# Decode step with attention and MLP on one core: the last 64 rows of w1 are fetched in another order of rows

## The chip, the core and the metric

The kernel runs on one core of a Trainium2 chip. The metric is device time of one execution in microseconds (us). Five compute queues matter: TensorE (PE, with its weight loads PEld), VectorE (DVE), ScalarE (ACT), GpSimd (POOL) and SyncE (SP), which here issues nearly all transfers. 16 DMA engines move the data.

## What is computed

```python
xn = layernorm(x)                                  # x: 4 x 576, bf16
A  = attention(xn, k_cache, v_cache, wq, wo)       # 32 query heads, 16 KV heads, the last 2048 positions of the cache
h  = gelu(layernorm(xn) @ w1)                      # w1: 576 x 576
g  = four quarters of h, each shifted along the sequence, joined
x1 = xn + g @ w2                                   # w2: 576 x 576
B  = x1 + gelu(layernorm(x1) @ w3) @ w4            # w3: 576 x 4608, w4: 4608 x 576
out = x + A + B
```

There are four batch rows, each with one position. With one position the shifts move everything out, so the joined quarters are zeros (`hs_inT` is a tile of zeros), and the product with w1 is computed though nothing reads its values.

## The kernel before

The data are 32 MB of K, 32 MB of V (16 transfers of 2 MB each) and the weights. The order on each queue is written out by hand: every operation is added with a key, and an engine's operations run in the order of their keys (`add`, `add_dma`, `emit_program`). Waits are on semaphores; each transfer adds 16 to its own one when it is complete, and w1's two transfers share one that must reach 32.

SP issues in this order (line 202 issues all of them): wq in two transfers (512 rows, then the last 64), w1 in two, w2 in two, w3 in two, w4 in two pieces (lines 268 to 276), then K 0 and 1, then K 2 once the query projection is done (`q`, line 358), K 3 (K 4 and later wait until a slot is free), then 15 pieces of V, the last of V, and wo in five pieces of 12, 10, 7, 2 and 1 rows a partition. All run through one queue of the 16 DMA engines.

Each weight with 576 rows is split. The first 512 rows lie four to a partition. The last 64 rows are cut in halves, so that 128 partitions get one half row each: `rag_src` (line 204) views rows 512 to 575 as 128 rows of half the width, half row 2r + h to partition 2r + h. For w1 a half row is 288 elements of bf16, 576 bytes, and the tile is `w1rag`. The other operand must match this layout: after each layernorm (`ln_ops`) two copies on DVE (lines 314 and 315) spread the last 64 elements of the normalized row over `ragsrc`, to the even places for h = 0 and to the odd places for h = 1, zeros elsewhere. TensorE transposes them (line 325), and `pe_hh` (line 393) multiplies them with `w1rag` behind the four products of the first 512 rows. Index 0 of `ragsrc` belongs to wq, 1 to w1, 2 to w3.

The attention then works on one K transfer at a time: transposes on TensorE (line 496), copies out of PSUM on DVE and ACT (480, 479), scores (503); then softmax, the transposed probabilities (530 to 543), the products with V (567) with their folding (573 to 591), and the output projection with wo (386, 64 matmuls at the end), which is copied out on DVE and ACT (628, 629).

Of the kernel before, what the change touches and what calls it, by code (L numbers as in the profile page):

```python
# [34 lines left out]
def bass_parallel_sum__sliding_block_cached__mixer_s_mlp__decode_kernel(  # L35
    nc, A_x, A_k_cache, A_v_cache, A_wq, A_wo, B_x, B_w1, B_w2, B_w3, B_w4, out
):
    B, Sq, D = A_x.shape
# [25 lines left out]
    with ExitStack() as ctx:  # L64
        def sb(name, shape, dt):
            return ctx.enter_context(nc.sbuf_tensor(name, shape, dt))

        def sem(name):
            return ctx.enter_context(nc.semaphore(name))
# [20 lines left out]
        def cut(n):  # L90
            nonlocal _o
            _o += n
            return ktb[:, _o - n:_o]
        w1main = cut(4 * D).rearrange("p (r n) -> p r n", r=4)
        w1rag = cut(HALF)
# [22 lines left out]
        ragsrc = sb("ragsrc", [B, 3, 2, 128], BF16)  # L118
# [72 lines left out]
        def add(engine, emit, waits=(), sig=None, key=0.0, inc=None):  # L191
            seqc[0] += 1
            prog[engine].append(Op(emit, waits, sig, key, seqc[0], inc))

        def add_dma(pairs, skey, waits=(), key=0.0, engine="sp"):
            if skey not in S:
                S[skey] = sem("s_" + "_".join(str(k) for k in (skey if isinstance(skey, tuple) else (skey,))))
            dma_count[skey] = dma_count.get(skey, 0) + 16 * len(pairs)

            def emit(e):  # L200
                for o_, i_ in pairs:
                    e.dma_start(o_, i_).then_inc(S[skey], 16)  # L202
            add(engine, emit, waits, None, key)
            return ("dma", skey, dma_count[skey])

        def rag_src(w_ap):
            return w_ap[512:576, :].rearrange("r (h n) -> (r h) n", h=2)

        for n in range(NB):
            ev_val[f"T{n}"] = ("T", n + 1)  # L210
        for c in range(-1, NC - 1):
# [51 lines left out]
        for x in range(2):  # L263
# [3 lines left out]
        ev_x = add_dma([(x_sb[:], x2)], "x", (), -100, engine="act")  # L267
        ev_wq = [add_dma([(kring[:, 2 * UE:4 * UE], A_wq[0:512, :].rearrange("(p r) n -> p (r n)", r=4))], "wq", (), -50),
                 add_dma([(wqrag, rag_src(A_wq))], "wqr", (), -49)]
        ev_w1 = add_dma([(w1main, B_w1[0:512, :].rearrange("(p r) n -> p r n", r=4)), (w1rag, rag_src(B_w1))], "w1", (), -48)  # L270
        ev_w2 = add_dma([(w2main, B_w2[0:512, :].rearrange("(p r) n -> p r n", r=4)), (w2rag, rag_src(B_w2))], "w2", (), -47)
        ev_w3 = add_dma([(vring[:, 0:4 * F], B_w3[0:512, :].rearrange("(p r) n -> p (r n)", r=4)), (w3rag, rag_src(B_w3))],
                        "w3", (), -46)
# [17 lines left out]
        ev_wo, WOR, a = [], [], 0  # L291
# [10 lines left out]
        def ln_ops(idx, src, dst, first_waits, tag, k0):  # L302
            add("dve", lambda e: (e.bn_stats(out=stats[:, idx, 0, :], in_=src[:, 0:HALF]),
                                  e.bn_stats(out=stats[:, idx, 1, :], in_=src[:, HALF:D]))[1],
                waits=first_waits, sig=f"{tag}_st", key=k0)
            add("dve", lambda e: e.bn_aggr(out=mv[:, idx, :], in_=stats[:, idx].rearrange("p a s -> p (a s)")),
                waits=[f"{tag}_st"], sig=f"{tag}_mv", key=k0 + 0.01)
            add("act", lambda e: e.activation(out=sd[:, idx:idx + 1], in_=mv[:, idx, 1:2], func=ACTF.Sqrt, bias=EPS, scale=1.0),
                waits=[f"{tag}_mv"], sig=f"{tag}_sd", key=k0 + 0.02)
            add("dve", lambda e: e.reciprocal(out=rstd[:, idx:idx + 1], in_=sd[:, idx:idx + 1]),  # L310
                waits=[f"{tag}_sd"], sig=f"{tag}_rstd", key=k0 + 0.03)
            add("dve", lambda e: e.tensor_scalar(out=dst[:], in0=src[:], scalar1=mv[:, idx, 0:1], scalar2=rstd[:, idx:idx + 1],  # L312
                                                 op0=ALU.subtract, op1=ALU.mult), waits=[f"{tag}_rstd"], sig=f"{tag}_n", key=k0 + 0.04)
            add("dve", lambda e: (e.tensor_copy(out=ragsrc[:, idx, 0, 0:128:2], in_=dst[:, 512:D]),
                                  e.tensor_copy(out=ragsrc[:, idx, 1, 1:128:2], in_=dst[:, 512:D]))[1],  # L315
                waits=[f"{tag}_n", "rag_zero"], sig=tag, key=k0 + 0.05)

        def pe_xT(src, idx):
            def f(e):
# [9 lines left out]
        def pe_zero(e):  # L329
# [3 lines left out]
            return ins  # L333

        ln_ops(0, x_sb, xn_bf, [ev_x], "ln1", -40)
        ln_ops(1, xn_bf, xn2_bf, ["ln1"], "ln2", -30)
        for idx, (src, tag, dst) in enumerate(((xn_bf, "ln1", xnT), (xn2_bf, "ln2", xn2T))):
            add("pe", pe_xT(src, idx), waits=["ident_bf", tag], sig=f"xT{idx}", key=-50 + idx)
            add("dve", lambda e, dst=dst, idx=idx: e.tensor_copy(out=dst[:], in_=XTps[idx]), waits=[f"xT{idx}"], sig=f"xnT{idx}",  # L339
                key=-29 + idx * 0.1)  # L340
# [36 lines left out]
        for k in range(2):  # L377
            for b in range(B):
                for g in range(2):
                    add("dve", lambda e, k=k, b=b, g=g: e.tensor_copy(  # L380
                            out=qp_out[:, b, 2 * k + g].rearrange("p (j n) y -> p j n y", j=2),
                            in_=QTps[:, k, :, 2 * g:2 * g + 2, b].rearrange("p (n y) j -> p j n y", y=2)),
                        waits=["qTp1", "qpad_zero"], sig=f"qT{8 * k + 2 * b + g}", key=-10 + 0.1 * k)
# [20 lines left out]
        for h in range(2):  # L404
            cs = slice(HALF * h, HALF * (h + 1))
            add("pe", pe_hs(h), waits=[ev_w2, "hs_inT"] + (["x1a"] if h else []), sig=f"hs{h}", key=-23 + h)
            add("dve", lambda e, cs=cs: e.tensor_tensor(out=x1_bf[:, cs], in0=HSps, in1=xn_bf[:, cs], op=ALU.add),
                waits=[f"hs{h}"], sig="x1" if h else "x1a", key=-7 + 0.1 * h)
        ln_ops(2, x1_bf, x1n_bf, ["x1"], "ln3", -6)
        add("dve", lambda e: e.tensor_tensor(out=t1[:], in0=x_sb[:], in1=x1_bf[:], op=ALU.add), waits=["x1"], sig="t1", key=-5.9)  # L410
        add("act", lambda e: (e.activation(out=hh_sb[0:B, :], in_=HHps[0], func=ACTF.Gelu_apprx_tanh),
                              e.activation(out=hh_sb[32:32 + B, :], in_=HHps[1], func=ACTF.Gelu_apprx_tanh))[1],
            waits=["hT", "ln3_sd"], sig="gelu_h", key=-5.9)
# [38 lines left out]
        for k in range(3):  # L452
            add("pe", pe_h2(k), waits=[ev_w3] + (["x1nT", "gelu_h", "h2_zero"] if k == 0 else []), sig=f"h2_{k}", key=-18 + k)
            add("act", lambda e, k=k: e.activation(out=h2_sb[:, k], in_=H2ps[k], func=ACTF.Gelu_apprx_tanh), waits=[f"h2_{k}"],
                sig=f"gelu2_{k}", key=-5 + 0.1 * k)
# [3 lines left out]
            waits=["h2Tp"], sig="h2T", key=-4.5)  # L459
# [17 lines left out]
        def evac(n):  # L477
            if n % 8 in ACT_EVAC:
                return "act", lambda e: e.activation(out=ktbuf[:, n % NKT], in_=tb[n % 4], func=ACTF.Copy)  # L479
            return "dve", lambda e: e.tensor_copy(out=ktbuf[:, n % NKT], in_=tb[n % 4])  # L480

        for n in range(NB):
            c, k = n // NBLK, n % NBLK
            if k == 0:
                add("dve", lambda e, c=c: e.tensor_copy(out=Qs[:, c % N_CB, :], in_=Qpad_t[:, 128 * (4 * CH[c][0] + CH[c][1]):][:, 0:128]),
                    waits=["qT15"] + ([f"SC{c - N_CB}"] if c >= N_CB - 1 else []), key=n)
            eng, f = evac(n)
# [11 lines left out]
        def emit_SC(e, k):  # L499
# [11 lines left out]
            waits=["rmax"], sig="negb", key=KS + 0.05)  # L511
        for q in range(4):
            add("act", lambda e, q=q: e.activation(out=P_sb[:, q, :], in_=Sps[:, q, :], func=ACTF.Exp,
                                                   bias=negb[:, 0:1], scale=scale, accum_out=rs4[:, q:q + 1]),
                waits=["negb"], sig=f"exp{q}", key=KS + 0.1 + 0.01 * q)
# [18 lines left out]
        for q in range(4):  # L534
            k0 = KS + 0.2 + 0.1 * q
            add("dve", dve_mask(q), waits=[f"exp{q}", "mask4"], sig=f"P4_{q}", key=k0)
            add("pe2", pe_PT(q), waits=[f"P4_{q}"] + (["sel_bf"] + [f"E{NB - 1 - k}" for k in range(4)] if q == 0 else []),
                sig=f"PTp{q}", key=k0)
            add("act", lambda e, q=q: e.activation(out=PTx[:, q, :], in_=ps[:, 4 + q, :], func=ACTF.Copy),  # L539
                waits=[f"PTp{q}"], sig=f"PTx{q}", key=k0 + 0.05)  # L540
            add("pe2", lambda e, q=q: e.matmul(ps[:, q, :], lhsT=permT_bf[:], rhs=PTx[:, q, :], start=True, stop=True),
                waits=[f"PTx{q}", "permT_bf"], sig=f"PTy{q}", key=k0 + 0.11)
            add("act", lambda e, q=q: e.activation(out=PT_t[:, 512 * q:512 * (q + 1)], in_=ps[:, q, :], func=ACTF.Copy),  # L543
                waits=[f"PTy{q}"], sig=f"PT{q}", key=k0 + 0.16)
# [3 lines left out]
            waits=["rinv", "ident_f"], sig="diag", key=KS + 0.82)  # L548
        add("pe2", lambda e: e.matmul(rinvps, lhsT=ones_f[:], rhs=diag[:], start=True, stop=True),
            waits=["diag", "ones_f", "PT3"], sig="rinvp", key=KV + 0.5)  # L550
        add("dve", lambda e: e.tensor_copy(out=rinvB[:].rearrange("p (c u e) -> p c u e", u=NU, e=2),
                                           in_=rinvps.rearrange("p (u c e) -> p c u e", u=NU, e=2)),
            waits=["rinvp"], sig="rinvB", key=KV + 1.5)
# [26 lines left out]
        for c in range(NC):  # L580
            b, gq = CH[c]
# [5 lines left out]
                waits=[f"PV{c}", "maskd"], key=KV + 2 * c + 0.6, inc=(("FF", k), 1))  # L587
            add("dve", lambda e, c=c: e.tensor_reduce(out=acc[:, c % NVS, :], in_=tmp[c % 2].rearrange("p t d -> p d t"), axis=AX.X, op=ALU.add),  # L588
                waits=[f"F{c}"] + ([f"fold{c - NVS}"] if c >= NVS else []), key=KV + 2 * c + 0.7, inc=(("AA", k), 1))
            cs = slice(32 * b + 8 * gq, 32 * b + 8 * gq + 8)  # L590
            add("dve", lambda e, k=k, cs=cs: e.tensor_tensor(out=OTn[:, cs], in0=OTps[k], in1=rinvB[:, cs], op=ALU.mult),  # L591
                waits=["rinvB", f"fold{c}"], key=KV + 2 * c + (2.75 if c < NC - 1 else 3), inc=(("OO", k), 1))
# [11 lines left out]
            waits=["OR"], sig="ORT", key=KE + 0.3)  # L604
# [66 lines left out]
        e = nc.tensor  # L671
# [62 lines left out]
```

## Time and profile before

| | us |
|---|---|
| median of 3 runs | 215.27 (215.07 to 215.28) |
| profiled execution | 215.12 |
| its span | 213.9 |

In the profile, busy time is the time in which an engine executes; for the DMA engines it is the mean share over all 16. "The chain that ended last" follows the work back from the last instruction, at each step to what released it. A stretch of the span lists each engine's busy time (with the number of instructions), the granted TensorE clock, the busy share of the DMA engines and the rate in GB/s. A DMA issue is listed with its size and the time from issue to landing. In counts of packets, those under 512 B are nearly all the small packets with which an engine reports its share of a transfer as done.

### The profile page before, as it was taken

How to read it: one execution, taken by the hardware profiler on the slowest of the kernel's cores; microseconds unless marked ns; L12 is line 12 of the kernel's file. 1: busy time of each engine (PE TensorE's matmuls, PEld its weight loads, DVE VectorE, ACT ScalarE, POOL GpSimd, SP SyncE). 2: the span in 40 equal slices, each digit the busy share in tenths (PEclk: the TensorE clock that was granted, in tenths of full speed). 3: DMA queues.
4: the chain of work that ended last, by engine and by line, in shares of the span. 5: the costliest groups of instructions: out<-in, count | busy, mean ns of one | idle time of the engine just before them, and what ended most of it. 6: DMA issues, size and time to landing. Idle time of an engine off the chain costs nothing.

```text
span 213.9 us, 4528 instructions
## 1 busy us (share of the span) xinstructions
PE 151.6 (71%) x1984; PEld 96.9 (45%) x1987; DVE 116.8 (55%) x240; ACT 64.3 (30%) x78; POOL 12.7 (6%) x20
## 2 busy tenths in 40 slices
PE   2038478578999999999999971788444455555964
PEld 0013126337878877888887860434111122212332
DVE  4962720015767776667677666759934333334520
ACT  2001032003666666556666665810000000000000
POOL 8950000000000000000000000000000000000000
PEclk9999958889999999999999999557855555555699
DMA  7999989999999999999999999999999999999993
GB/s 277 411 385 494 427 376 440 429 417 420 435 429 420 423 438 426 423 426 438 427 420 429 435 426 420 434 429 417 429 435 423 426 432 435 423 426 432 426 400 122
DMA packets 6802, 88.64 MB, mean 414 GB/s; under 512 B 764, under 2 KB 1160, under 8 KB 1928
## 3 DMA queue, kind: packets, MB, share of 16 engines
q1 hardware_dynamic: 6776, 88.50, 97.7%
q8 instruction: 7, 0.11, 0.2%
q14 instruction: 3, 0.02, 0.0%
q10 hardware_dynamic: 16, 0.01, 0.0%
HBM read 88.49 MB, written 0.00 MB: 414 GB/s over the span
## 4 chain that ended last, share of the span: by engine, by line
DMA 68%; PE 17%; DVE 9%; ACT 3%; issue 1%; SPq 1%
DMA kring<-in_A_k_cache_dram 41%; DMA kring<-in_A_wo_dram 16%; DMA vring<-in_A_v_cache_dram 10%; PE ps L496 7%; DVE xn_bf L312 4%; PE ps L567 3%; PE ps L503 2%; PE ps L358 2%; SPq L202 1%; DVE rmax L509 1%; DVE ktb L521 1%; ACT ktb L539 1%; ACT PT L543 1%; DMA x_sb<-in_A_x_dram 1%; PE ps L386 1%
## 5 line engine op out<-in xcount | busy, mean ns | idle before, releaser
L480 DVE COPY ktb<-ps 128x1024 bf16<-128x1024 bf16 x80 | 53.8, 690 | 24.7 <-PE ps L496 24.2
L496 PE MATMUL ps<-perm_bf,kring 128*128 128x128 bf16 x1024 | 62.6, 219 | 3.0 <-DMA kring<-in_A_k_cache_dram 2.1
L496 PEld LDWEIGHTS ps<-perm_bf,kring 128*128 128x128 bf16 x1024 | 57.2, 98 | 12.6 <-issue 9.8
L479 ACT ACTIVATE ktb<-ps 128x1024 bf16<-128x1024 bf16 x48 | 49.2, 1024 | 31.6 <-PE ps L496 30.8
L567 PE MATMUL ps<-vring,ktb 128*32 128x512 bf16 x240 | 25.8, 575 | 23.2 <-DMA vring<-in_A_v_cache_dram 23.2
L585 DVE TENSOR_TENSOR ktb<-ps,maskd 128x512 f32<-128x512 f32 x16 | 11.0, 690 | 29.6 <-PE ps L567 29.5
L629 ACT ACTIVATE out_sb<-ps 4x288 bf16<-4x288 f32 x1 | 0.4, 402 | 72.4 <-PE ps L386 72.4
L567 PEld LDWEIGHTS ps<-vring,ktb 128*32 128x32 bf16 x240 | 7.1, 121 | 30.9 <-issue 27.3
L503 PE MATMUL ps<-ktb,Qs 128*32 128x512 bf16 x272 | 17.8, 382 | 1.2 <-ACT ktb L479 1.2
L588 DVE TENSOR_REDUCE acc<-ktb 128x128 f32<-128x512 f32 x16 | 16.4, 1028 | 0.5
L573 PEld LDWEIGHTS ps<-sel,acc 128*128 128x128 f32 x34 | 7.3, 268 | 14.6 <-issue 8.8
L573 PE MATMUL ps<-sel,acc 128*128 128x8 f32 x34 | 8.8, 331 | 2.5 <-DVE OTn L591 2.5
L503 PEld LDWEIGHTS ps<-ktb,Qs 128*32 128x32 bf16 x272 | 5.8, 95 | 6.7 <-DVE ktb L480 1.4
L322 PE MATMUL ps<-ident_bf,xn_bf 4*128 4x4 bf16 x8 | 0.6, 170 | 11.4 <-DVE xnT L339 8.9
L386 PE MATMUL ps<-vring,h2T_sb 128*4 128x288 bf16 x72 | 6.4, 348 | 2.5 <-DMA vring<-in_B_w_dram 2.5
L559 DVE TENSOR_TENSOR ktb<-PT,mU_bf 128x512 bf16<-128x512 bf16 x16 | 6.6, 416 | 2.1 <-ACT PT L543 2.1
L312 DVE TENSOR_SCALAR xn_bf<-xn_bf,mv,rstd 4x576 bf16<-4x576 bf16 x1 | 7.4, 7430 | 0.0
L245 POOL MEMSET ktb<- 128x8192 bf16 x1 | 6.9, 6925 | 0.0
L530 PE MATMUL ps<-sel_bf,ktb 128*128 128x32 bf16 x64 | 2.4, 189 | 5.5 <-DVE ktb L521 5.5
L386 PE MATMUL ps<-kring,ORT 128*4 128x288 bf16 x64 | 4.4, 286 | 2.4 <-DMA kring<-in_A_wo_dram 1.8
L322 PEld LDWEIGHTS ps<-ident_bf,xn_bf 4*128 4x128 bf16 x8 | 0.4, 112 | 12.3 <-DVE ragsrc L315 9.0
L386 PEld LDWEIGHTS ps<-vring,h2T_sb 128*4 128x4 bf16 x72 | 3.6, 100 | 5.1 <-DMA vring<-in_B_w_dram 2.7
(117 smaller groups left out, 96.4 us busy)
## 6 DMA issues: line engine op xcount, KB each, us to landing
kring<-in_A_k_cache_dram SPq DMA_DIRECT2D x16, 2048.0 KB, 14.7
vring<-in_A_v_cache_dram SPq DMA_DIRECT2D x15, 2048.0 KB, 22.4
vring<-in_B_w_dram SPq DMA_DIRECT2D x1, 4608.0 KB, 24.9
kring<-in_A_wq_dram SPq DMA_DIRECT2D x1, 4096.0 KB, 12.4
vring<-in_B_w_dram SPq DMA_DIRECT2D x1, 3456.0 KB, 34.7
kring<-in_A_v_cache_dram SPq DMA_DIRECT2D x1, 2048.0 KB, 26.7
ktb<-in_B_w_dram SPq DMA_DIRECT2D x3, 576.0 KB, 14.5
vring<-in_B_w_dram SPq DMA_DIRECT2D x1, 1728.0 KB, 38.3
```

Source lines behind the costliest of these rows:

```text
L245: P(lambda e: e.memset(ktb[:, NKT // 2 * 1024:NKT * 1024], 0.0), key=-92, inc=(("E", LB - 2), 1))
L312: add("dve", lambda e: e.tensor_scalar(out=dst[:], in0=src[:], scalar1=mv[:, idx, 0:1], scalar2=rstd[:, idx:idx + 1], op0=ALU.subtract, op ...
L386: return e.matmul(ACC[h], lhsT=lhsT, rhs=rhs, start=start, stop=stop, tile_position=(0, 32 * h), skip_group_check=True)
L479: return "act", lambda e: e.activation(out=ktbuf[:, n % NKT], in_=tb[n % 4], func=ACTF.Copy)
L480: return "dve", lambda e: e.tensor_copy(out=ktbuf[:, n % NKT], in_=tb[n % 4])
L496: ins = e.transpose(tb[j % 4][:, t, :], kslot_t(k)[:, 8 * kb + t, :], perm_bf[:])
L503: ins = e.matmul(Sps[32 * u:32 * u + 32, q, :].rearrange("p (t i) -> p t i", t=16), lhsT=Qs[:, k, 32 * u:32 * u + 32], rhs=ktgrp[:, (4 * k ...
L559: return lambda e: e.tensor_tensor(out=PTpad[:, c % NVS], in0=PTv[:, :, cc, :].unsqueeze(2).to_broadcast([128, NT, NU, 2]), in1=mU_bf[:].u ...
L567: ins = e.matmul(ps[32 * j:32 * j + 32, PVb[k], :], lhsT=PTpad[:, k, 4 * g:4 * g + 4].rearrange("p t u e -> p (t u e)"), rhs=v[:, 512 * g: ...
L573: e.matmul(OTps[k], lhsT=acc[:, k, :], rhs=sel8[:], start=True, stop=True, skip_group_check=True).then_inc(S["FO"], 1)
L585: add("dve", lambda e, c=c: e.tensor_tensor(out=tmp[c % 2], in0=ps[:, PVb[c % NVS], :].rearrange("p (t d) -> p t d", t=4), in1=maskd[:].un ...
L588: add("dve", lambda e, c=c: e.tensor_reduce(out=acc[:, c % NVS, :], in_=tmp[c % 2].rearrange("p t d -> p d t"), axis=AX.X, op=ALU.add), wa ...
```

## The change

The source of w1's last 64 rows is viewed through one more rearrangement: the 128 half rows are taken as 16 groups of 8, and walked with the place in the group outermost (8), the group next (16), the 288 elements last. The destination is the same tile of 128 partitions. So partition 16a + b gets half row 8b + a. To match, the two copies that fill `ragsrc` for index 1 write the elements in the order of these half rows: for each h, 4 x 16 elements. Half row 8b + a is half h = a mod 2 of row 4b + a div 2, so each h reads its elements with a stride of 4 and writes runs of 16. Indices 0 and 2 are filled as before, and the transfers of all other weights stay.

```diff
+        def rag8_src(w_ap):
+            return rag_src(w_ap).rearrange("(b a) n -> a b n", a=8)
...
-        ev_w1 = add_dma([(w1main, B_w1[0:512, :].rearrange("(p r) n -> p r n", r=4)), (w1rag, rag_src(B_w1))], "w1", (), -48)
+        ev_w1 = add_dma([(w1main, B_w1[0:512, :].rearrange("(p r) n -> p r n", r=4)), (w1rag, rag8_src(B_w1))], "w1", (), -48)
...
-            add("dve", lambda e: (e.tensor_copy(out=ragsrc[:, idx, 0, 0:128:2], in_=dst[:, 512:D]),
-                                  e.tensor_copy(out=ragsrc[:, idx, 1, 1:128:2], in_=dst[:, 512:D]))[1],
-                waits=[f"{tag}_n", "rag_zero"], sig=tag, key=k0 + 0.05)
+            def rag(e):
+                ins = None
+                for h in range(2):
+                    if idx == 1:
+                        ins = e.tensor_copy(out=ragsrc[:, 1, h].rearrange("q (a x b) -> q x a b", a=4, x=2)[:, h],
+                                            in_=dst[:, 512:D].rearrange("q (b a) -> q a b", a=4))
+                    else:
+                        ins = e.tensor_copy(out=ragsrc[:, idx, h, h:128:2], in_=dst[:, 512:D])
+                return ins
+            add("dve", rag, waits=[f"{tag}_n", "rag_zero"], sig=tag, key=k0 + 0.05)
```

## The prediction

> **What bounds the kernel now.** I read the busy shares first, then the DMA queues, the chain that ended last, and the stretches by time.
>
> ```profile
> span 213.9 us, 4528 instructions
> PE 151.6 (71%) x1984; PEld 96.9 (45%) x1987; DVE 116.8 (55%) x240; ACT 64.3 (30%) x78; POOL 12.7 (6%) x20
> ...
> DMA packets 6802, 88.64 MB, mean 414 GB/s; under 512 B 764, under 2 KB 1160, under 8 KB 1928
> ## 3 DMA queue, kind: packets, MB, share of 16 engines
> q1 hardware_dynamic: 6776, 88.50, 97.7%
> ```
>
> No compute engine is above 71%. The queue that SP feeds (q1) keeps the 16 DMA engines busy for 97.7% of the span: the kernel is a stream of 88.5 MB. The chain of waits says the same: 68% of it is DMA, and its end is this.
>
> ```profile
> 150.30 20.86 DMA vring<-in_A_v_cache_dram
> ...
> 175.56 34.97 DMA kring<-in_A_wo_dram
> 210.54 0.04 issue
> 210.58 1.44 PE ps L386 x20
> 212.01 0.44 DVE out_sb L628
> ```
>
> The last transfers (wo) are issued at 174.5 to 176.5 and land some 35 us later, because they stand behind all that was issued before. So the end is set by how long an engine needs for its own share of everything queued. The stretches show how the 16 engines end (the last two columns are the busy share of the DMA engines and GB/s):
>
> ```profile
> 180.00:200.00 20.00, 11.28 (x76) 4.63 (x77) 8.33 (x16) 0.00 (x0) 0.00 (x0) 0.50 1.00 426
> 200.00:205.00 5.00, 4.08 (x31) 1.58 (x30) 2.27 (x5) 0.00 (x0) 0.00 (x0) 0.88 1.00 421
> ...
> 208.00:209.00 1.00, 0.83 (x14) 0.61 (x16) 0.00 (x0) 0.00 (x0) 0.00 (x0) 1.00 0.97 392
> 209.00:210.00 1.00, 0.56 (x10) 0.17 (x4) 0.00 (x0) 0.00 (x0) 0.00 (x0) 1.00 0.62 247
> 210.00:211.00 1.00, 0.42 (x8) 0.32 (x10) 0.00 (x0) 0.00 (x0) 0.00 (x0) 1.00 0.43 161
> 211.00:212.00 1.00, 0.97 (x16) 0.47 (x12) 0.00 (x0) 0.00 (x0) 0.00 (x0) 1.00 0.03 12
> ```
>
> Until 209 all are busy; then the share falls to 0.62 and 0.43. So about half of the engines are out of work near 209.5, and the others run to about 211. All engines have the same bytes, yet the late ones are some 1.5 us behind, and the kernel waits for them: PE starts its last 20 matmuls at 210.58, when the third piece of wo has landed on its slowest engine. A microsecond given to a late engine is a microsecond of the kernel; one given to an early engine costs nothing up to 1.5 us.
>
> **The change, part by part.**
>
> *The transfer's split.* The 128 rows of 576 B (72 KB) stay; the source is now walked as 8 x 16 rows. Do the shapes decide how many engines take part? The page's counts answer for the rows here. Every engine that takes part in a transfer posts a completion packet of a few bytes. The page lists 47 issues with 128 destination rows (16 of K, 16 of V, 5 of wo, 10 of the other weights) and 3 with 4 rows (x and two of out). 47 x 16 + 3 x 4 = 764, which is the page's count of packets under 512 B. So 128 rows went to 16 engines and 4 rows to 4. A transfer whose one side begins with 8 and the other with 128 does not occur here; I take it that the smaller side decides, and that 8 engines get 16 rows each where 16 had 8. [...]
>
> *The price of a row.* The stretch from 14.5 to 16 us holds this transfer whole:
>
> ```profile
> DMA packets 278, 0.62 MB, mean 412 GB/s; under 512 B 32, under 2 KB 160, under 8 KB 278
> ...
> q1 hardware_dynamic: 278, 0.62, 104.2%
> ```
>
> 160 - 32 = 128 are its rows, 32 are completions, and 118 are rows of 4608 B of w1 and w2. Their time is 1.042 x 16 x 1.5 us = 25.0 us. The stretch 16 to 16.5 holds only 47 rows of 4608 B at 104.6%, so 1.046 x 16 x 0.5 / 47 = 178 ns each. 25.0 - 118 x 0.178 = 4.0 us remain for 128 rows: 31 ns a row with its share of completions, or 0.25 us for each engine's 8 rows. The lower bound is the rate of the long rows: 576/4608 x 178 = 22 ns, 0.18 us for 8. The upper bound is the nearest slow small packets, those of x: in the first 5 us its queue has 8 packets (4 of 1152 B, 4 completions) at 0.5% of 16 x 5 us, so 0.1 us for each row. I take 31 ns, since these are the very rows; the new order of rows may only change it within these ends. [...]
>
> So eight engines have 0.25 us more to do and eight have 0.25 us less. From then on the queue never runs dry (share 1.00 in every stretch from 60 to 205 us), so the shift is neither hidden nor made up: it stands at the end as it was made at 15 us. The end moves by +0.25 us if an engine among the last ones is one of the loaded eight, and by -0.25 us if all the last ones are in the other eight. Nothing in this profile numbers the engines. The late ones are several and end close together, so one loaded engine among them is enough for the later end.
>
> *The queue of SP.* The transfer is issued near 2.2 us; the same number of transfers is issued. Eight engines hold 8 more entries. SP's issue of the second piece of w4 lasts from 5.39 to 11.18 (5.79 us, against 0.5 us for others), as if it waited for room, while the first 4 MB drain. With 8 more entries ahead it may wait for 8 more rows, at 178 ns some 1.4 us; K's first two transfers are queued behind it. Then SP stands anyway:
>
> ```profile
> SPq L202 <- PE ps L358: 5.8, 1, 5.8
> ```
>
> This wait for the query projection, before the third K transfer, covers 1.4 us. Were it gone, that transfer (issued at 19.45, landed at 63.5) would still have some 39 us, since its own 2 MB need only the last 4.9 us. Cost: nothing.
>
> *When w1 is complete.* It lands some 14.2 us after its issue, so near 16.5, and 0.25 us later now. Its first reader, L393, starts at 20.59, after the transposes of q: 4 us of cover.
>
> *The copies on DVE.* Still two copies of 64 elements, now 4 x 16 with other strides. The old ones took 0.19 us each (L314, L315); other small copies take 0.15 to 0.17 (L380, L339), so I bound each at -0.04 to +0.19 us, and take 0. They stand ahead of the copy to xnT, so q and the third K transfer would move with them; the same 39 us cover that. PE has the same instructions.
>
> **Sum.** +0.25 us on the last engines and nothing else: 215.12 (the profiled execution: span 213.9 and 1.2 around it) + 0.25 = 215.37. The median of the runs is 215.27, 0.15 above that execution; from it the sum would be 215.52. I forecast **215.4**, no change that counts: 0.2% (0.43 us) is about what a measurement of this kernel can tell from no change.
>
> **Rivals.**
>
> 1. *The last engines are all among the eight relieved* (0.32): 215.12 - 0.25 = 214.87, or 215.02 by the median. For it: the 0.62 and 0.43 of the tail fit an even split into eight early and eight late engines. [...]
> 2. *Still 16 engines* (0.10): the 128 rows of the destination alone decide; 215.27. For it: all transfers of before fit this reading as well.
> 3. *Slower, by dear rows* (0.09): an engine's successive reads are now 8 x 576 = 4608 B apart, and it writes other partitions than in all other transfers. If a row costs as much as one of x, 0.1 us, a loaded engine needs 16 x 0.1 - 0.25 = 1.35 us more: 216.5. It counts as slower from 16p - 0.25 = 0.43, a row of 42 ns, if a loaded engine is last; if only early ones are loaded, the 1.5 us of lead swallows it. Against it: 31 ns for the same rows now.
>
> The forecast has 0.45; 0.04 are left for what I don't see, split evenly.
>
> **How the numbers follow.** Forecast and the first two rivals lie between 214.87 and 215.52, all within 0.2%: 0.87; I leave 0.02 of it to each side for noise. Slower: 0.09 + 0.02 + 0.02 = 0.13; faster: 0.02 + 0.02 = 0.04; same 0.83. The range takes in both signs, the price of a row from 22 to 42 ns, and the 0.2 us between runs: 214.8 to 215.8. The likeliest case's own range is 215.3 to 215.55.
>
> **What would show it.** The completions: under 512 B 756 instead of 764 if eight engines take part, 764 if sixteen. The stretch with the 576 B rows: longer by about 0.25 us, with some engines already on w2. The tail: by the forecast the shares after 209 us stretch to later, the third piece of wo landing near 210.8; by the first rival they draw together and it lands near 210.3. SP's long issue of w4 may grow to some 7 us, with the third K transfer still issued near 19. The forecast is wrong if DMA share falls below 1.00 in the middle, or if K, V or wo transfers take longer each.

## The result, and the profile after

| | before | after |
|---|---|---|
| median of 16 runs | 215.28 us | 215.73 us |
| ratio, 95% interval | | 1.0029 [1.0016, 1.0042] |
| profiled span | 213.9 us | 214.4 us |
| third piece of wo lands | 210.54 us | 211.06 us |

The changed kernel is slower: by 0.45 us between the medians, by 0.62 us (0.34 to 0.90) by the ratio, by about 0.5 us in the profiles. Four of the 16 runs after and one of the 16 before took some 1.3 us longer than the others, which draws the ratio up more than the medians; without them the means differ by 0.44 us. The forecast was 215.4 and no change that counts.

The page of the changed kernel, its span, packets and the queue of SP:

```profile
span 214.4 us, 4528 instructions
...
DMA packets 6794, 88.64 MB, mean 413 GB/s; under 512 B 756, under 2 KB 1152, under 8 KB 1920
...
q1 hardware_dynamic: 6768, 88.50, 97.6%
```

756 packets under 512 B instead of 764: the transfer posts 8 completions and not 16, so eight engines carry it. Bytes and the share of q1 stay. The end of the chain (start, length, what):

```profile
176.11 34.95 DMA kring<-in_A_wo_dram
211.06 0.04 issue
211.11 1.44 PE ps L396 x20
212.54 0.43 DVE out_sb L638
```

It is the chain of before, each piece about 0.53 us later, and no piece is longer. The DMA engines' tail (busy share and GB/s last):

```profile
208.00:209.00 1.00, 0.30 (x6) 0.23 (x8) 0.00 (x0) 0.00 (x0) 0.00 (x0) 1.00 0.96 396
209.00:210.00 1.00, 1.00 (x18) 0.57 (x14) 0.00 (x0) 0.00 (x0) 0.00 (x0) 1.00 0.79 311
210.00:211.00 1.00, 0.09 (x2) 0.00 (x0) 0.00 (x0) 0.00 (x0) 0.00 (x0) 1.00 0.49 186
211.00:212.00 1.00, 0.89 (x16) 0.65 (x18) 0.00 (x0) 0.00 (x0) 0.00 (x0) 1.00 0.05 17
```

After 209 the shares sum to 1.33 instead of 1.08. The early engines end later (0.79 for 0.62), and so do the late ones: more was added than a shift from eight engines to the other eight, which would leave the sum as it was. Where it was added shows around the transfer itself, in half microseconds, first of before, then of after:

```profile
15.00:15.50 0.50, 0.50 (x8) 0.14 (x4) 0.00 (x0) 0.00 (x0) 0.00 (x0) 1.00 1.12 418
15.50:16.00 0.50, 0.50 (x8) 0.14 (x4) 0.00 (x0) 0.00 (x0) 0.00 (x0) 1.00 1.04 423
16.00:16.50 0.50, 0.50 (x12) 0.16 (x8) 0.00 (x0) 0.00 (x0) 0.00 (x0) 1.00 1.05 433
```

```profile
15.00:15.50 0.50, 0.50 (x8) 0.14 (x4) 0.00 (x0) 0.00 (x0) 0.00 (x0) 1.00 1.13 398
15.50:16.00 0.50, 0.50 (x8) 0.14 (x4) 0.00 (x0) 0.00 (x0) 0.00 (x0) 1.00 1.04 326
16.00:16.50 0.50, 0.50 (x12) 0.19 (x8) 0.00 (x0) 0.00 (x0) 0.00 (x0) 1.00 0.98 396
```

The engines are as busy (1.04), but move 326 GB/s instead of 423. So packets take longer, and not those of the changed transfer alone. The counts from 14.5 to 16.5 us say whose, before and after:

```profile
DMA packets 325, 0.83 MB, mean 417 GB/s; under 512 B 32, under 2 KB 160, under 8 KB 325
...
q1 hardware_dynamic: 325, 0.83, 104.3%
```

```profile
DMA packets 302, 0.77 MB, mean 383 GB/s; under 512 B 24, under 2 KB 152, under 8 KB 302
...
q1 hardware_dynamic: 302, 0.77, 104.1%
```

Before: 1.043 x 16 x 2 us = 33.4 us; less 4.0 us for the 128 rows of 576 B (31 ns each), 29.4 us for 325 - 160 = 165 rows of 4608 B, 178 ns each. After: 33.3 us; less 4.0 us, 29.3 us for 302 - 152 = 150 rows, 195 ns each. Single packets in the two traces bear out the split: the 576 B rows take 29 ns in both, but some 40 rows of 4608 B in this stretch take 200 to 300 ns. Each of the 49 that began between 15.36 and 16.06 us took 187 ns or more, and eight engines have no time for 49 such rows there, so the slowing was not on the eight alone; I take it that all engines were slowed. That is 150 x 17 ns = 2.6 us of engine time, 0.16 us for each of 16 engines on the mean. With the 0.25 us of 8 more rows it makes 0.41 us on a loaded engine (by equal shares, one of the eight that carry 16 of the rows; the other eight, the relieved ones, carry none).

### The profile page after: what moved, and what is told of

It is laid out like the page before. It is cut to its first block, busy times and chain, and to the rows that moved or that the text cites. A ratio compares the mean times of both kernels' runs of the same rounds, so it can differ in the third digit from the quotient of the medians.

```text
span 214.4 us, 4528 instructions
## 1 busy us (share of the span) xinstructions
PE 151.6 (71%) x1984; PEld 96.9 (45%) x1987; DVE 116.8 (54%) x240; ACT 64.3 (30%) x78; POOL 12.7 (6%) x20
## 4 chain that ended last, share of the span: by engine, by line
DMA 68%; PE 17%; DVE 9%; ACT 3%; issue 1%; SPq 1%
DMA kring<-in_A_k_cache_dram 41%; DMA kring<-in_A_wo_dram 16%; DMA vring<-in_A_v_cache_dram 10%; PE ps L506 7%; DVE xn_bf L315 4%; PE ps L577 3%; PE ps L513 2%; PE ps L368 2%; SPq L202 1%; DVE rmax L519 1%; DVE ktb L531 1%; ACT ktb L549 1%; ACT PT L553 1%; PE ps L396 1%; DMA x_sb<-in_A_x_dram 1%
## 6 DMA issues: line engine op xcount, KB each, us to landing
kring<-in_A_k_cache_dram SPq DMA_DIRECT2D x16, 2048.0 KB, 14.7
vring<-in_A_v_cache_dram SPq DMA_DIRECT2D x15, 2048.0 KB, 22.4
```

## The experiments

The theory after the result: two terms, 0.25 us for 8 more rows on eight engines of which one ends late, and 0.16 us for a slowing of the rows beside the transfer. Rivals: the copies on DVE have a part; only the first term is real and the rest is chance; and, for the second term, different causes. Kernels measured together share their runs of before. The rows' mean is worked out as above, from 14.5 to 16.5 us.

| run | outermost dimension, destination | completions | rows of 4608 B, ns | median us | before us | ratio [95%] |
|---|---|---|---|---|---|---|
| after | 8, 128 partitions | 756 | 195 | 215.73 | 215.28 | 1.0029 [1.0016, 1.0042] |
| e1 | 8, transfer alone | 756 | 195 | 215.69 | 215.32 | 1.0012 [0.9992, 1.0033] |
| e2 | 128, copies alone | 764 | 178 | 215.26 | 215.32 | 0.9990 [0.9970, 1.0009] |
| e3 | 8, w1 and w2 | 748 | 201 | 216.32 | 215.32 | 1.0033 [1.0015, 1.0050] |
| e4 | 16, strided | 764 | 188 | 215.46 | 215.32 | 1.0005 [0.9986, 1.0025] |
| e5 | 8, blocks | 756 | 197 | 215.74 | 215.33 | 1.0017 [1.0006, 1.0028] |
| e6 | 4, blocks | 752 | 201 | 216.24 | 215.33 | 1.0046 [1.0031, 1.0061] |
| e7 | 2, blocks | 750 | not uniform | 215.66 | 215.33 | 1.0018 [1.0005, 1.0031] |
| e8 | 16, blocks | 764 | 186 | 215.42 | 215.33 | 1.0002 [0.9986, 1.0017] |
| e9 | 128, every other row | 764 | 178 | 215.36 | 215.32 | 0.9998 [0.9983, 1.0014] |
| e10 | 32, to 32 partitions | 764 | 215 | 215.61 | 215.32 | 1.0014 [1.0000, 1.0028] |
| e11 | no w1 | 732 | | 213.66 | 215.32 | 0.9924 [0.9898, 0.9950] |
| e12 | no w1, no w2 | 700 | | 215.43 | 215.32 | 0.9978 [0.9949, 1.0007] |
| e13 | 32, 128 partitions | 765 | 178 | 215.32 | 215.38 | 0.9995 [0.9977, 1.0013] |
| e14 | 64, to 64 partitions | 764 | 213 | 215.77 | 215.38 | 1.0023 [0.9999, 1.0046] |
| e15 | wq, 8 | 756 | | 220.28 | 215.38 | 1.0214 [1.0186, 1.0241] |
| e16 | wq, 16 | 764 | | 216.56 | 215.33 | 1.0063 [1.0036, 1.0090] |
| e17 | wq, 32 | 764 | | 215.26 | 215.33 | 0.9987 [0.9972, 1.0002] |

Differences of 0.1 to 0.4 us are at the edge of these intervals, and medians and ratios don't agree to the last tenth; the durations of rows in the traces carry the argument there, the times where they are far apart (e3, e6, e11, e15, e16).

### e1 and e2: one part of the change at a time

e1: before, with this line changed (and `rag8_src` added); e2: the changed kernel with the old source.

```diff
-... (w1rag, rag_src(B_w1))], "w1", (), -48)     # e1
+... (w1rag, rag8_src(B_w1))], "w1", (), -48)
-... (w1rag, rag8_src(B_w1))], "w1", (), -48)    # e2
+... (w1rag, rag_src(B_w1))], "w1", (), -48)
```

> The changed transfer with the old copies on DVE; so w1's last 64 rows meet the wrong elements of xn2, in a product that nothing reads. The theory (the transfer loads eight DMA engines and everything else is hidden) expects the time of the changed kernel, 215.7, 756 completions, and w2's rows of 4608 B at up to 300 ns near 15.5 us. The rival (the copies on DVE have a part in it) expects a time between 215.3 and 215.6.

> The new copies on DVE with the old transfer; the same product meets the wrong rows. The theory expects the time of before, 215.3, and 764 completions. The rival (the copies count) expects 215.4 to 215.7.

e1 took 215.69 with rows of 4608 B as slow as after the change (195 ns), e2 215.26 with rows of 178 ns. The transfer is the cause; the copies are not.

### e3: two transfers by 8

```diff
-... (w2rag, rag_src(B_w2))], "w2", (), -47)
+... (w2rag, rag8_src(B_w2))], "w2", (), -47)
```

> The last 64 rows of w2 come by an outermost dimension of 8 as well (their order is changed; they are multiplied with zeros). Theory A (a loaded engine is last, and each such transfer costs it 8 rows, 0.23 us, and a slowing of the rows beside it, some 0.2 us) expects as much again as the change brought: 216.1 to 216.3. Theory B (the rows alone count, the rest of the measured 0.45 is chance) expects 0.23 more than the changed kernel: 215.9. If the last engine were a relieved one, it would be below the changed kernel.

216.32, so 1.00 us above before: the second transfer costs at least as much as the first. Theory A holds, and chance is out. The sign is settled too: a loaded engine is last.

### e4, e5 and e8: is it the strided source?

```diff
+            return rag_src(w_ap).rearrange("(b a) n -> a b n", a=16)      # e4
+            v = w_ap[508:576, :].rearrange("r (h n) -> (r h) n", h=2)     # e5
+            return v.rearrange("(a b) n -> a b n", a=8)[:, 0:16, :]
+            v = w_ap[504:576, :].rearrange("r (h n) -> (r h) n", h=2)     # e8
+            return v.rearrange("(a b) n -> a b n", a=16)[:, 0:8, :]
```

> The source is walked with an outermost dimension of 16 and 8 rows behind it, 16 x 576 = 9216 B apart: strided reads as in the change, but 764 completions, so 8 rows for each of 16 engines (the copies are the old ones, so the product that nothing reads meets the wrong rows). If the load on eight engines and what it does on the destination side is the cause, the time is that of before, 215.3, and w2's rows stay at 178 ns. If the strided reading of the source slows the rows beside it, w2's rows take 200 to 300 ns near 15.5 us, and the time is some 0.2 us above before, 215.45.

> Outermost dimension 8, but each of the eight engines reads one run of 16 half rows that follow each other (9216 B, then a gap of one half row, so that the dimensions don't merge); for this the block starts at half row 1016 of w1, so the product that nothing reads gets other rows. 756 completions. Theory A (two terms: 8 rows more on the loaded engines, 0.23 us, and a slowing of the rows beside it that comes from engines reading the same block of the source in turns) expects w2's rows at 178 ns and 215.5. Theory B (the slowing comes from what eight engines write: partitions that belong to others in all other transfers) expects w2's rows at 200 to 300 ns and the time of the changed kernel, 215.7.

> A control: an outermost dimension of 16 with runs of 8 half rows (4608 B) and a gap of one half row between them; 764 completions, 8 rows on each engine, and engines don't share a block of the source. Theory A and B expect 215.3 as before and w2's rows at 178 ns. If the gap alone (not the sharing) slowed the rows beside it, 215.4 to 215.5.

e5 reads each engine's rows from one run, and w2's rows are as slow as with the change (197 ns, 215.74). So engines that share a block of the source are not the cause: theory A of that expectation fell. e4 and e8 have 8 rows on each engine and a slowing of half the size (188 and 186 ns; 0.14 and 0.09 us by the medians, which is within the noise): a load on eight engines is not needed for it. No trace shows which partitions an engine fills. I take it that each gets an equal share of the outermost dimension; then e4, e5, e8 and the change have in common that an engine fills 8 or 16 partitions that follow each other. They also have in common that the source is not read as one block.

### e6 and e7: which engines are late

As e5, with `w_ap[510:576, :]`, `a=4` and `[:, 0:32, :]`, or `w_ap[511:576, :]`, `a=2` and `[:, 0:64, :]`.

> The same with an outermost dimension of 4 (runs of 32 half rows): 32 rows instead of 8 on four engines, 752 completions. If the engine that is last, or one at most 0.2 us ahead of it, is among the four: 24 x 29 ns = 0.70 us more, 215.9 to 216.0. If the four include none of the late ones, the end is set by a relieved engine or by an early one that is now later: 215.0 to 215.3. If a slowing comes with few engines that write many partitions (theory B), 0.1 to 0.2 us more than either.

> The same with an outermost dimension of 2 (runs of 64 half rows): 64 rows instead of 8 on two engines, 750 completions. If the last engine is one of the two: 56 x 29 ns = 1.62 us more, 216.9. If the two are among the early ones (1.5 to 2 us ahead), their lead takes up the 1.62 us and the others are relieved of 0.25 us: 215.0 to 215.4. A value between tells the lead of the later of the two.

e6: 24 x 29 ns = 0.70 and, with rows of 201 ns, 147 x 23 / 16 = 0.21 us, together 0.91; measured 0.91 between the medians (to the hundredth that is luck). So a late engine is among the four. e7: 1.62 us more on two engines, but 0.33 us more in time: these two had a lead of at least about 1.3 us, and the tail's early half is real. The completions (752, 750) follow the outermost dimension.

### e9: gaps in the source with two dimensions

```diff
+            v = w_ap[448:576, :].rearrange("r (h n) -> (r h) n", h=2)
+            return v.rearrange("(a x) n -> a x n", x=2)[:, 0, :]
```

> Control for e10 and for the reading: the 128 half rows of 576 B are every other half row of w1's last 128 rows, one to a partition, so the transfer keeps two dimensions as before (128 x 288), while the source is no longer one block (the product that nothing reads gets other rows). If the slowing comes from how the source is read (gaps), w2's rows take about 200 ns as in e8 and the time is 215.4. If it comes from which engine writes which partitions, they stay at 178 ns and the time is 215.3.

Rows of 178 ns and 215.36: gaps alone slow nothing.

### e10, e13 and e14: the destination

e13 has three dimensions, the outermost 32, and writes all 128 partitions. e10 and e14 read in the same way, without the gap between groups, and write four (two) rows to each of 32 (64) partitions in a free part of `vring`.

```diff
+            return v.rearrange("(a b x) n -> a b x n", b=4, x=2)[:, :, 0, :]      # e10, v as in e9
+        w1nar = vring[0:32, 4 * F + W4R * D:4 * F + W4R * D + 4 * HALF].rearrange("p (b n) -> p b n", b=4)
+            v = w_ap[416:576, :].rearrange("r (h n) -> (r h) n", h=2)             # e13
+            return v.rearrange("(a b x) n -> a b x n", b=5, x=2)[:, 0:4, 0, :]
```

> The same half rows as e9, four to a partition, written to 32 partitions only (in a free part of vring; the product that nothing reads takes w2's last rows instead). 764 completions, 8 rows of 576 B on each of 16 engines. If the slowing comes from writes that gather on the way to few partitions, w2's rows are slowed more than in e8, on the engines that write there: 215.5 to 215.8. If the number of rows an engine has is all that counts besides the gaps of the source, the time is that of e9 and e8, 215.3 to 215.4.

> The reads of e10 (groups of 4 half rows, every other one, outermost dimension 32, so three dimensions and 8 rows in sequence for each of 16 engines; a gap between groups keeps the dimensions apart), but written to 128 partitions, one row each (the product that nothing reads gets other rows). If the destination makes the slowing, it is as in e8: w2's rows at about 200 ns for a while, 215.4. If the way of reading makes it, it is as in e10: rows of up to 390 ns, 215.6.

> As e10, with two half rows to each of 64 partitions instead of four to each of 32. If the slowing goes with how many rows meet on a partition or a group of them, it lies between e8 and e10: 215.45 to 215.55. If it needs only several rows to one partition, as e10: 215.6; if it does not depend on the destination, as e13.

From 14.5 to 16.5 us, e10 and then e13:

```profile
DMA packets 298, 0.71 MB, mean 355 GB/s; under 512 B 32, under 2 KB 160, under 8 KB 298
...
q1 hardware_dynamic: 298, 0.71, 105.4%
```

```profile
DMA packets 330, 0.83 MB, mean 414 GB/s; under 512 B 35, under 2 KB 167, under 8 KB 330
...
q1 hardware_dynamic: 330, 0.83, 103.6%
```

355 against 414 GB/s: as many rows for each engine, read in the same pattern, and only the destination (and the gap between groups; e9 had gaps and no slowing) differs. So the destination alone can make the slowing. Rows of w2 take 215 ns in e10, single ones up to 390, and 178 in e13. I had expected of e13 what e8 showed, and it showed no slowing at all. The reading that fits, though no trace shows an engine's partitions: with an outermost dimension of 32 they come in blocks of 4, and not of 8 or 16. 64 partitions (e14: 213 ns, +0.39 us) are no better than 32 (e10: +0.29 us), where I had expected something between.

By what means 64 partitions cost what 32 do (213 and 215 ns), no run shows. Nor does one show why, over 128 partitions, the outermost dimensions 128 and 32 left w2's rows at 178 ns (e9, e13), 16 took them to 186 and 188 (e8, e4) and 8 to 195 and 197 (the change, e5).

### e15, e16 and e17: the same on long rows

The change's two edits are moved from w1 to wq, whose rows have 4096 B, with `a=8`, `16` or `32`, and the copies of index 0 to match:

```diff
-                 add_dma([(wqrag, rag_src(A_wq))], "wqr", (), -49)]
+                 add_dma([(wqrag, rag8_src(A_wq))], "wqr", (), -49)]
-                    if idx == 1:
+                    if idx == 0:
```

> The change's two edits moved to wq: its last 64 rows (rows of 4096 B, 159 ns) come by an outermost dimension of 8, with the copies of index 0 to match; w1 as before. Each loaded engine has 8 x 0.159 = 1.27 us more. If the slowing stays as small as for w1 (0.1 to 0.2 us), 216.7 to 216.8; if it goes with the bytes (7 times those of w1's rows, so about 1 us), 217.5 or more; if long rows don't cause it, 216.6.

> As e15 with an outermost dimension of 16: 764 completions, 8 rows of 4096 B on each of 16 engines as before, each engine filling 8 partitions that follow each other. [...] If only the load on eight engines did it in e15, 215.3.

> As e15 with an outermost dimension of 32: 764 completions, 8 rows on each engine, blocks of 4 partitions as in e13. By the blocks: no slowing, 215.3. If any strided source with long rows slows the stream, as much as e16.

Stretches from 13 to 16 us, with the rate last: e15, e16, e17.

```profile
13.00:14.00 1.00, 0.13 (x4) 0.13 (x5) 0.79 (x4) 0.00 (x0) 0.72 (x4) 1.00 1.05 156
14.00:15.00 1.00, 1.00 (x18) 0.42 (x21) 0.17 (x1) 0.00 (x0) 0.00 (x0) 1.00 1.09 191
15.00:16.00 1.00, 1.00 (x16) 0.37 (x12) 0.00 (x0) 0.00 (x0) 0.00 (x0) 1.00 0.90 144
```

```profile
13.00:14.00 1.00, 0.00 (x0) 0.00 (x0) 0.97 (x4) 0.00 (x0) 0.48 (x4) 1.00 0.94 221
14.00:15.00 1.00, 0.97 (x14) 0.51 (x18) 0.21 (x2) 0.00 (x0) 0.00 (x0) 1.00 1.14 247
15.00:16.00 1.00, 1.00 (x16) 0.31 (x12) 0.00 (x0) 0.00 (x0) 0.00 (x0) 1.00 0.90 341
```

```profile
13.00:14.00 1.00, 0.00 (x0) 0.00 (x0) 0.97 (x4) 0.00 (x0) 0.57 (x4) 1.00 1.04 427
14.00:15.00 1.00, 0.89 (x14) 0.51 (x18) 0.29 (x3) 0.00 (x0) 0.00 (x0) 1.00 1.02 416
15.00:16.00 1.00, 1.00 (x12) 0.28 (x8) 0.00 (x0) 0.00 (x0) 0.00 (x0) 1.00 1.01 395
```

The shares are near 1 everywhere, while the rate in the first of these microseconds is 156, 221 or 427 GB/s. e16 and e17 move the same bytes to the same partitions, with 8 rows for each engine as before, and differ in the outermost dimension alone (16 or 32, and with it the order of rows in the source): 216.56 against 215.26. From 12 to 16 us e16 moves 0.47 MB less than e17, some 1.1 us at 425 GB/s, and it is 1.2 us slower than before.

Single packets show where the time went, and here the transfer's own rows were slow too. wq's rows of 4096 B took 159 ns on the mean in before and e17, 249 in e16 and 347 in e15; the 256 rows of 4608 B behind them (w1 and w2) took 178, 208 and 313. For e16 that is (128 x 90 + 256 x 30) / 16 = 1.2 us for each engine, all of what was measured. For e15 it is (128 x 188 + 256 x 135) / 16 = 3.7 us, and with the load of 8 x 159 ns = 1.27 us it makes 4.9, as measured.

So the shape of the transfer is the cause of the second term, with no load on eight engines (e16) and with no change of the source's pattern (e10 against e13). That it works through the partitions which each engine fills fits all runs, and is an inference. The order of the source alone doesn't explain it: at 16 both a strided source (e4) and one read in runs (e8) slowed the rows, and e9 and e13, with gaps, did not.

### e11 and e12: what a microsecond of transfers is worth

e11 drops the line of w1's transfers, and `pe_hh` takes w2's rows; e12 drops w2's line too, and both products take w3's.

> Both transfers of w1 are left out, and the product that nothing reads uses w2's rows in place of w1's. Every engine has 8 rows of 4608 B (178 ns), 8 of 576 B (29 ns) and two completions (9 ns) less: 1.67 us. If the end is set by the engines' work alone, the time is 215.3 - 1.67 = 213.65. If a fixed wait near the start or the end sets a part of it, it is above 213.9.

> The transfers of w2 are left out too; the product with w2, whose other operand is zeros, uses rows of w3. By the engines' work 3.35 us less than before: 212.0. If the later start of that product (it waits for w3 now) delays V's first transfers or anything behind them, above 212.3.

e11 took 213.66 (expected 213.65): the end is set by the engines' work. It beats both kernels, and leaves out only what nothing reads. e12 missed by 3.4 us; its runs lie between 213.7 and 218.0 us, so its median says little, and the trace is that of one of 216.23 us. The product waits for w3 now, and everything behind it on PE starts later (L391 at 26.67 us, the same product before at 20.59). K's slots come free later, and the rate falls:

```profile
40.00:60.00 20.00, 16.19 (x230) 11.80 (x226) 5.37 (x12) 5.19 (x7) 0.00 (x0) 0.91 0.94 393
60.00:80.00 20.00, 20.00 (x347) 16.56 (x340) 14.20 (x26) 12.05 (x13) 0.00 (x0) 1.00 0.99 391
```

PE is busy for all of 60 to 80 us, and the rate of 392 instead of 427 GB/s over 40 us loses 3.3 us, about all that was saved. Only a part of that is an empty queue: the share falls to 0.94 in the first stretch (0.52 between 58 and 60 us). In the second it is 0.99, and single rows of 16 KB are slow, up to 1.9 us; why was not tried.

## Why the prediction was wrong, point by point

**The bound** was right. e11 gave back 1.66 us by the medians, of the 1.67 us that its rows cost an engine.

**Eight engines, and a late one among them** was right: 756 completions, and e3 and e6 grow with the load. The first rival (a relieved engine last) is out, and so is the second (still 16 engines).

**The price was the step that failed.** "I take 31 ns, since these are the very rows" held for the rows themselves: 29 ns each, in before and after. But 0.25 us was taken as the whole price. The rows of w2 beside them were left at 178 ns, and they took 195 on the mean: 0.16 us more for each engine on the mean. The term for what the transfer does to its neighbours was put at nothing, without a reason ("and nothing else"). The sum should have been about 0.4, at the edge of the 0.43 us that I took as what can be told from no change; the medians moved by 0.45, and the ratio's interval, about 0.28 us to each side, is clear of 1. The working priced a transfer by its own packets, in a trace where it stood among others on an equal footing. The sum asked how many engines a shape gives, and not which partitions each of them fills.

**The third rival** had the place (an engine "writes other partitions than in all other transfers"), but put the price on the transfer's own rows, at 0.1 us each. Here they were not dear, at 29 ns; their neighbours were. On wq's long rows (e15, e16) both were. By the same means a relieved engine saved 0.25 - 0.16 us, not 0.25, so the first rival's 214.87 would not have been reached either.

**SP's queue**: its two issues of w4 ended 0.80 us later (11.97 for 11.17 us), of the 1.4 us that I allowed. K's first two issues made up 0.5 us of it, and the wait for q, 5.5 us instead of 5.8, the rest. The third K transfer was issued at 19.42 us, 0.03 us earlier than before:

```profile
SPq L202 <- PE ps L368: 5.5, 1, 5.5
```

**The copies** took 0.18 us each instead of 0.19 (L321), and e2 shows no cost. **w1's landing** had its cover: no wait for it appears after either.

**The signs**: the tail grew later as forecast (0.79 and 0.49), but the landing at 211.06 and not 210.8 was the sign that a second term was missing. The two signs that were to show a wrong forecast stayed silent: the share did not fall in the middle (1.00 to 1.02 from 60 to 200 us), and K, V and wo transfers took 14.7, 22.4 and 35.0 us as before. The loss lay in about one microsecond near 15.5 us, at a share of 1.04.

## What to carry to other kernels

When the 16 DMA engines set the end, price a reshaped transfer by two questions: how many rows the most loaded engine gets, and what it does to the rows beside it, for which these runs point at the partitions that each engine fills. Here an outermost dimension of 32 or 128 over 128 partitions was free, 16 cost 0.1 us on 72 KB and 1.2 us on 512 KB, and 8 cost 0.4 and 4.9. A stretch in which the share stays near 1 and the rate falls (here 1.04, and 326 GB/s for 423) shows that packets take longer; the count of packets in it, and their durations, tell whose.

## What the runs showed of the hardware that I had not expected

- A transfer of 72 KB slowed the rows of others until half a microsecond after its own last row (15.54 us; rows of 187 ns and more began up to 16.06), and its own rows kept their 29 ns. The same shape on 512 KB held the stream at 144 to 206 GB/s for 6 us, and its own rows took 347 ns instead of 159.
- The cost went up faster than the bytes: 7 times the bytes (wq against w1, dimension 8) made 0.16 us of slowing into 3.7 us, 1.5 of it on the transfer's own rows. Why it isn't in proportion stays open; a longer overlap with the transfers on both sides was not tried.
- Two engines could take 1.62 us more work for 0.33 us of time (e7): the engines of this kernel end up to 2 us apart (the tail of before, from 209 to 211 us), on equal bytes by the 16 completions of each large transfer. What makes the late ones late was not tried. The traces hold a candidate: each has seven packets of 16 KB on another queue, of kind `instruction`. In before they took 1.03 to 1.10 us each, and five of them were followed at once by a row of 16 KB that took about 1.1 us instead of 0.61. One engine so loses an estimated 1.5 us each time, which is the lag of the late ones; that it is these engines that end last is not shown, since no packet in the traces bears an engine's number.
